# Turning the keys on VectorE instead of TensorE in a decode-attention kernel

## The chip, the cores and the metric

The kernel runs on one core of a Trainium2 chip. The core has TensorE (PE: matmuls and transposes, results into PSUM), VectorE (DVE), ScalarE (ACT), GpSimd (POOL) and the queues that issue transfers, here almost only SyncE's (SP). The metric is the device time of one execution in microseconds (us), the median of several runs; the profile is one execution of its own.

## The reference, cut to what matters

```python
def _A_ref(x, k_cache, v_cache, wq, wo):          # B=2, D=512, 32 query heads, 8 KV heads, Dh=128
    W = min(4096, max(256, Sk // 4))              # 4096: the last 4096 keys of 32768
    q = (x @ wq) ...                              # one position per batch entry
    k = jnp.repeat(k_cache[:, :, Sk - W:, :], 4, axis=1)
    v = jnp.repeat(v_cache[:, :, Sk - W:, :], 4, axis=1)
    p = _softmax(jnp.einsum("bhqd,bhkd->bhqk", q, k) * (Dh ** -0.5), axis=-1)
    return einsum("bhqk,bhkd->bhqd", p, v) ... @ wo
def _B_ref(x, W_gate, W_up, W_down):              # F = 1792
    gate = x @ W_gate; up = x @ W_up
    return (gate * (gate > 0) * up) @ W_down
xn = _layernorm(x)
return x + _A_ref(xn, ...) + _B_ref(xn, ...)
```

All data are float32. One token of each of two batch entries reads 4096 keys and 4096 values of eight KV heads, which with the weights makes 95 MB, each byte used once.

## The kernel before, in words

**Tiles and slots.** Attention goes in four groups g (batch entry b and half r of the KV heads, so four KV heads each), and each group in two pairs of heads, a = 0 and 1. One K tile and one V tile of 4 MB hold a pair (g, a). `load_kv` (L85) puts partition p = 2y + h: y counts 64 runs of 64 keys, h is the head of the pair; along a partition stand 64 keys (J) of 128 components. All large transfers (two halves of wq, W_gate, W_up, eight K, eight V, W_down, two parts of wo) go into one ring of four 4 MB slots (`load`, L69; RING = 4) and are issued in program order on SP's queue (L71, L449). A load therefore waits until the tile four loads before it has been read for the last time, and everything behind it on that queue waits with it. The order is: wq, wq, W_gate, W_up, K(0,0), K(0,1), then K(g,a), V(g-1,a) for g = 1 to 3, then V(3,0), V(3,1), W_down, wo.

**Program order.** `manual_schedule` (L66) keeps the instructions of each engine in the order in which the program emits them; there is no planner. An instruction that waits holds all that stand behind it on its engine.

**Keys and scores.** A score product needs the components of a key on the partitions. `transposes` (L248) turns a K tile on PE in 64 products of 128x128 with the identity (L256), four of them into one PSUM bank, and `evacuate` (L244) copies each bank to SBUF, alternately on ACT and DVE (L245), setting the two heads apart on the way. `scores` (L262) multiplies: per half tile s1, 2 heads x 4 column groups of 32 (L269), every one with 128 components, 32 query columns and 512 keys. The 32 columns of `qz` are zero except for the four query heads that belong there. All scores of a group gather in one PSUM bank, `ss[g]`.

**Softmax.** `softmax` (L275) is a generator whose steps `kwork` (L375) puts between the transposes of the next group's first K tile: maximum on DVE (L278), a transpose of it on PE, DVE steps, four small products `nm_ps` (L293), one exponential of 128x1024 on ACT (L302; each score is written twice), eight PE transposes of the probabilities (L313), two DVE products with the mask `own` that keeps a head's own half (L314), and the sums `lp` and their reciprocal (L320, L322).

**Values and the end.** `values` (L326) makes 16 products per V tile (L333) and a DVE mask (L339); `gather` (L346) adds pairs on PE, `finish` (L355) sums on DVE and divides, `spread_heads` (L363) moves heads to where the product with wo takes them. After the last group come W_down, wo, the sums and the store (L413 to L464).

Of the kernel before, what the change touches and what calls it, by code (L numbers as in the profile page):

```python
# [20 lines left out]
def kernel(  # L21
# [12 lines left out]
    nc = tc.nc  # L34
# [76 lines left out]
    NSLOT = C * S1  # L111
    qz = const.tile([P, NG, NSLOT * 36], F32, name="qz")
    nc.gpsimd.memset(qz, 0.0)
    ones = const.tile([1, 1], F32, name="ones")
# [7 lines left out]
    spread = const.tile([HR, NE, HR, NE], F32, name="spread")  # L122
    nc.gpsimd.memset(spread, 0.0)
    for e in range(NE):
        nc.gpsimd.tensor_copy(spread[:, e, :, e], ident[0:HR, 0:HR])
# [18 lines left out]
    by_h = const.tile([P, NP, HK], F32, name="by_h")  # L144
    nc.vector.tensor_reduce(
        out=by_h, in_=ident.rearrange("p (q a s k) -> p a k q s", q=Q, a=NP, s=S1), op=ALU.add, axis=AX.XY
    )

    half_of = const.tile([P, 2], F32, name="half_of")
    nc.vector.tensor_reduce(  # L150
        out=half_of, in_=ident.rearrange("p (y h) -> p h y", h=2), op=ALU.add, axis=AX.X
    )
    own = const.tile([P, 2, REP], F32, name="own")
    nc.vector.tensor_copy(own, half_of[:, :, None].to_broadcast([P, 2, REP]))

# [18 lines left out]
    xn = const.tile([B, D], F32, name="xn")  # L174
# [29 lines left out]
    for r in range(R):  # L204
        qs = work.tile([P, 512], F32, name=f"qs{r}", tag="qs")
        (nc.vector.tensor_copy if r else nc.scalar.copy)(qs, q_ps[r])
        qt = ps_kt.tile([P, REP, C, 16, B], F32, name=f"qt{r}", tag="kt")
        for i in range(REP):
            nc.tensor.transpose(  # L209
                qt[:, i].rearrange("p c s b -> p (c s b)"), qs[:, i * P:(i + 1) * P], ident  # L210
            )
        for b in range(B):
            dst = qz[:, r * B + b].rearrange("p (a s h k) -> p a s h k", a=NP, s=S1, h=2)
            for h in range(2):
                nc.vector.tensor_copy(  # L215
                    dst[:, :, :, h, 0:REP], qt[:, :, h::2, 0:S1, b].rearrange("p i a s -> p a s i")
                )

# [12 lines left out]
    gr = work.tile([P, FQ], F32, name="gr", tag="gr", bufs=1)  # L231
# [7 lines left out]
    HW = W // S1  # L239
    ss, pts, rls = {}, {}, {}  # L240
    kts, osb = {}, {}
    turn = [0]

    def evacuate(dst, src):  # L244
        (nc.vector.tensor_copy if turn[0] % 2 else nc.scalar.copy)(dst, src)  # L245
        turn[0] += 1

    def transposes(g, a, s1, kt_in):  # L248

        kt = ktp.tile([P, 2, HW], F32, name=f"kT{g}_{a}_{s1}", tag="kT")  # L250
        kts[g, a, s1] = kt
        for n in range(2 * Q):
            pk = ps_kt.tile([P, 512], F32, name=f"pk{g}_{a}_{s1}_{n}", tag="kt")
            for u in range(4):
                j = 8 * Q * s1 + 4 * n + u
                nc.tensor.transpose(pk[:, u * P:(u + 1) * P], kt_in[:, j * P:(j + 1) * P], ident)  # L256
            evacuate(
                kt[:, :, n * 256:(n + 1) * 256], pk.rearrange("p (y h) -> p h y", h=2),
            )
            yield  # L260

    def scores(g, a, s1):  # L262
        if (a, s1) == (0, 0):
            ss[g] = ps_s.tile([P, 512], F32, name=f"s{g}", tag="s")
        kt = kts.pop((g, a, s1))
        for h in range(2):
            n = (a * S1 + s1) * 2 + h
            for q in range(Q):
                nc.tensor.matmul(  # L269
                    ss[g][32 * q:32 * q + 32, :], qz[:, g, 32 * n:32 * n + 32],  # L270
                    kt[:, h, q * 512:(q + 1) * 512],
                    start=(a == 0 and s1 == 0 and h == 0), stop=(a == NP - 1 and s1 == S1 - 1 and h == 1),
                )

    def softmax(g):  # L275

        m = work.tile([P, 1], F32, name=f"m{g}", tag="m")
        nc.vector.tensor_reduce(out=m, in_=ss[g], op=ALU.max, axis=AX.X)  # L278
        yield
        mt = ps_1.tile([1, P], F32, name=f"mt{g}", tag="misc")  # L280
        nc.tensor.transpose(mt, m, ident)
        mx = work.tile([1, NP, HK], F32, name=f"mx{g}", tag="mx")
        nc.vector.tensor_reduce(
            out=mx, in_=mt.rearrange("p (q a s k) -> p a k q s", q=Q, a=NP, s=S1), op=ALU.max, axis=AX.XY
        )
        mb = work.tile([1, NP, S1, HK], F32, name=f"mb{g}", tag="mb")
        nc.vector.tensor_scalar(
            mb, mx[:, :, None, :].to_broadcast([1, NP, S1, HK]), -SCALE, None, op0=ALU.mult
        )
        yield  # L290
        nm_ps = ps_1.tile([P, 1], F32, name=f"nm_ps{g}", tag="misc")
        for q in range(Q):
            nc.tensor.matmul(  # L293
                nm_ps[32 * q:32 * q + 32, :], mb.rearrange("p a s k -> p (a s k)"), ones, start=True, stop=True
            )
        nm = work.tile([P, 1], F32, name=f"nm{g}", tag="nm")
        nc.vector.tensor_copy(nm, nm_ps)  # L297

        p = work.tile([P, 512, 2], F32, name=f"p{g}", tag="p", bufs=1)
        l = work.tile([P, 1], F32, name=f"l{g}", tag="l")  # L300
        both = ss[g][:, :, None].to_broadcast([P, 512, 2])
        nc.scalar.activation(p, both, AF.Exp, bias=nm, scale=SCALE, accum_out=l)  # L302
        yield
        yield
        yield

        pts[g] = work.tile([P, 2, Q * NP * S1, 4, HK], F32, name=f"pt{g}", tag="pt")
        pv = p.rearrange("r y h -> r (y h)")
        for jh in range(2):
            pp = ps_kt.tile([P, 4, P], F32, name=f"pp{g}_{jh}", tag="kt")  # L310
            for u in range(4):
                lo = (4 * jh + u) * P
                nc.tensor.transpose(pp[:, u], pv[:, lo:lo + P], ident)  # L313
            nc.vector.tensor_tensor(  # L314
                pts[g][:, jh].rearrange("p n u k -> p u n k"), pp.rearrange("p u (n k) -> p u n k", k=HK),
                own.rearrange("p h i -> p (h i)")[:, None, None, :].to_broadcast([P, 4, Q * NP * S1, HK]), op=ALU.mult,
            )
            yield
        lp = ps_1.tile([HR, 1], F32, name=f"lp{g}", tag="misc")
        nc.tensor.matmul(lp, by_h.rearrange("p a k -> p (a k)"), l, start=True, stop=True)  # L320
        rls[g] = work.tile([HR, 1], F32, name=f"rl{g}", tag="rl")
        nc.vector.reciprocal(rls[g], lp)  # L322

    ons = {}

    def values(g, a, v):  # L326
        o = ps_1.tile([P, 512], F32, name=f"o{g}_{a}", tag=f"o{a}")
        for s1 in range(S1):
            for jh in range(2):
                for q in range(Q):  # L330
                    n = (q * NP + a) * S1 + s1
                    lo = (8 * Q * s1 + 8 * q + 4 * jh) * P
                    nc.tensor.matmul(  # L333
                        o[32 * q:32 * q + 32, :],
                        pts[g][:, jh, n].rearrange("p u k -> p (u k)"), v[:, lo:lo + 512],
                        start=(s1 == 0 and jh == 0), stop=(s1 == S1 - 1 and jh == 1),
                    )
        ons[a] = work.tile([P, 4, P], F32, name=f"on{g}_{a}", tag="on")
# [16 lines left out]
    def finish(g):  # L355
# [5 lines left out]
        nc.vector.tensor_scalar(osb[r][:, b], od, rls[g], 2.0, op0=ALU.mult, op1=ALU.mult)  # L361

    def spread_heads(r):  # L363
        op = ps_1.tile([P, NJ, B], F32, name=f"op{r}", tag="misc")
        for e in range(NE):
            nc.tensor.matmul(  # L366
                op, spread[:, e].rearrange("h k e -> h (k e)"),
# [5 lines left out]
    pend = []  # L373

    def kwork(g, a, kt_in, others=()):  # L375

        others = list(others)
        for s1 in range(S1):
            for n, _ in enumerate(transposes(g, a, s1, kt_in)):
                if n > 1 and others and next(others[0], "end") == "end":  # L380
                    others.pop(0)
                if (a, s1, n) == (0, 0, 1) and pend:
                    scores(*pend.pop())
            if pend:
                scores(*pend.pop())
            pend.append((g, a, s1))
        for o in others:
            for _ in o:
                pass

    for a in range(NP):
        kwork(0, a, load_kv(k_cache, "k", 0, a))
    for g in range(1, NG):
        for a in range(NP):
            kt_in = load_kv(k_cache, "k", g, a)
            v_in = load_kv(v_cache, "v", g - 1, a)
            kwork(g, a, kt_in, [softmax(g - 1)] if a == 0 else [])
            if a:
                gather(g - 1, a - 1)
            elif g % B == 1 and g > 1:  # L400
                spread_heads((g - 2) // B)
            values(g - 1, a, v_in)
        gather(g - 1, NP - 1)
        finish(g - 1)
    g = NG - 1
    scores(*pend.pop())
    vin = [load_kv(v_cache, "v", g, a) for a in range(NP)]
    dw = load_down()
    for _ in softmax(g):
        pass  # L410
# [27 lines left out]
    for a in range(NP):  # L438
        values(g, a, vin[a])
        gather(g, a)  # L440
# [13 lines left out]
    yw = work.tile([P, D], F32, name="yw", tag="yw", bufs=1)  # L454
# [38 lines left out]
```

## Time and profile before

| what | before |
|---|---|
| median of 3 runs | 231.82 us (231.73 to 232.03) |
| the profiled execution | 231.71 us, its span 229.9 us |
| PE busy | 182.2 us in 1432 instructions |
| DVE busy | 73.3 us in 143 instructions |
| ACT busy | 46.6 us in 78 instructions |
| moved by DMA | 95.10 MB, mean 414 GB/s |
| mean granted TensorE clock | 0.925 |

The span goes from the first to the last instruction of the profiled execution; about 1.8 us of its time lie around it. Busy time is the time in which an engine had an instruction in work. In the lists of groups a row reads: line, engine, operation, tile written <- tiles read, partitions x elements, count | busy us, mean ns of one | idle us just before them and what ended it. The granted clock is the share of full speed that TensorE was given.

### The profile page before, as it was taken

The numbers are of one execution on the slowest core, as the hardware profiler recorded it, in microseconds if no ns is written. First come the engines' busy times: TensorE is split into PE (matmuls) and PEld (weight loads), VectorE is DVE, ScalarE is ACT, GpSimd is POOL, SyncE is SP. The second block draws the span as 40 slices with busy tenths as digits, with TensorE's granted clock in tenths as the row PEclk, the third lists the DMA queues.
The fourth block names the chain that finished last, engine by engine and source line by source line (L and its number), as shares of the span: only waits on it lengthen the run. The fifth ranks groups of instructions, "written<-read, shape, count | busy, mean of one in ns | idle before, by whom it ended". The sixth has DMA issues, their size and how long they took to land.

```text
span 229.9 us, 3250 instructions
## 1 busy us (share of the span) xinstructions
PE 182.2 (79%) x1432; PEld 96.0 (42%) x1432; DVE 73.3 (32%) x143; ACT 46.6 (20%) x78; POOL 3.8 (2%) x17
## 2 busy tenths in 40 slices
PE   0483970819999889998899699589999965889493
PEld 0430230219666573661583563248566213124011
DVE  2400021024444561641572441247244144111000
ACT  2000100004444550440351340025134002000001
POOL 6000000000000000000000000000000000000000
PEclk9998598576999999999999999889999996799799
DMA  7999999999999999999999999999999999999980
GB/s 274 456 433 391 464 409 466 399 445 450 422 408 450 436 410 423 448 428 413 439 450 419 416 446 442 410 422 456 425 410 436 445 422 430 428 445 405 420 339 14
DMA packets 3921, 95.10 MB, mean 414 GB/s; under 512 B 442, under 2 KB 450, under 8 KB 836
## 3 DMA queue, kind: packets, MB, share of 16 engines
q1 hardware_dynamic: 3896, 94.90, 96.4%
q8 instruction: 11, 0.18, 0.3%
q14 instruction: 2, 0.02, 0.0%
q10 hardware_dynamic: 12, 0.01, 0.0%
HBM read 94.90 MB, written 0.00 MB: 413 GB/s over the span
## 4 chain that ended last, share of the span: by engine, by line
PE 51%; DMA 41%; DVE 4%; ACT 2%; issue 1%; SPq 1%
DMA k<-in_A_k_cache_dram 25%; PE pk L256 23%; PE s L269 11%; DMA wo<-in_A_wo_dram 10%; PE o L333 9%; DMA wq<-in_A_wq_dram 5%; PE q_ps L198 3%; PE pp L313 2%; ACT p L302 2%; PE oa L350 2%; DVE kT L245 1%; PE op L366 1%; SPq L449 1%; DVE on L339 1%; PE nm_ps L293 0%
## 5 line engine op out<-in xcount | busy, mean ns | idle before, releaser
L256 PE MATMUL pk<-ident,k 128*128 128x128 f32 x512 | 67.3, 286 | 8.4 <-DMA k<-in_A_k_cache_dram 8.4
L256 PEld LDWEIGHTS pk<-ident,k 128*128 128x128 f32 x512 | 57.7, 146 | 24.6 <-issue 21.0
L245 ACT COPY kT<-pk 128x512 f32<-128x512 f32 x64 | 37.5, 586 | 100.1 <-PE pk L256 100.1
L245 DVE COPY kT<-pk 128x512 f32<-128x512 f32 x64 | 44.2, 691 | 37.9 <-PE pk L256 37.8
L333 PE MATMUL o<-v,pt 128*32 128x512 f32 x256 | 34.2, 627 | 0.0
L269 PE MATMUL s<-kT,qz 128*32 128x512 f32 x256 | 32.1, 607 | 0.0
L339 DVE TENSOR_TENSOR on<-o,own_u 128x512 f32<-128x512 f32 x8 | 5.5, 692 | 39.4 <-PE o L333 39.4
L333 PEld LDWEIGHTS o<-v,pt 128*32 128x32 f32 x256 | 8.9, 114 | 20.0 <-issue 19.9
L198 PE MATMUL q_ps<-wq,xnT 128*32 128x512 f32 x64 | 12.3, 940 | 4.3 <-DMA wq<-in_A_wq_dram 4.3
L269 PEld LDWEIGHTS s<-kT,qz 128*32 128x32 f32 x256 | 7.0, 111 | 13.2 <-issue 13.2
L350 PE MATMUL oa<-on,pick 128*16 128x512 f32 x16 | 8.2, 596 | 4.2 <-DVE on L339 4.2
L430 PE MATMUL yw_ps<-wo,oT 128*2 128x512 f32 x56 | 7.9, 703 | 3.9 <-DMA wo<-in_A_wo_dram 3.9
L186 PE MATMUL xt_ps<-rep,xn 2*128 2x32 f32 x16 | 3.7, 402 | 8.7 <-DVE rep L179 8.7
L225 PE MATMUL u_ps<-wu,xnT 128*32 128x448 f32 x32 | 5.2, 816 | 6.6 <-DMA wu<-in_B_W_up_dram 6.6
L198 PEld LDWEIGHTS q_ps<-wq,xnT 128*32 128x32 f32 x64 | 2.9, 163 | 12.9 <-issue 7.6
L313 PE MATMUL pp<-ident,p 128*128 128x128 f32 x32 | 5.5, 306 | 2.4 <-ACT p L302 1.5
L455 ACT COPY yw<-yw_ps 128x512 f32<-128x512 f32 x1 | 0.6, 586 | 33.3 <-PE yw_ps L430 33.3
L186 PEld LDWEIGHTS xt_ps<-rep,xn 2*128 2x128 f32 x16 | 3.6, 319 | 8.7 <-DVE rep L179 8.7
L302 ACT ACTIVATE p<-s,nm 128x1024 f32<-128x1024 f32 x4 | 4.5, 1115 | 13.0 <-DVE nm L297 12.9
L314 DVE TENSOR_TENSOR pt<-pp,own 128x512 f32<-128x512 f32 x8 | 5.5, 692 | 3.8 <-PE pp L313 3.7
L215 DVE COPY qz<-qt 128x16 f32<-128x16 f32 x8 | 0.8, 167 | 17.6 <-PE qt L209 17.6
L225 PEld LDWEIGHTS u_ps<-wu,xnT 128*32 128x32 f32 x32 | 1.3, 160 | 10.5 <-DMA wu<-in_B_W_up_dram 7.4
(72 smaller groups left out, 60.9 us busy)
## 6 DMA issues: line engine op xcount, KB each, us to landing
k<-in_A_k_cache_dram SPq DMA_DIRECT2D x8, 4096.0 KB, 29.1
v<-in_A_v_cache_dram SPq DMA_DIRECT2D x8, 4096.0 KB, 29.0
wq<-in_A_wq_dram SPq DMA_DIRECT2D x2, 4096.0 KB, 16.9
wo<-in_A_wo_dram SPq DMA_DIRECT2D x1, 4096.0 KB, 31.7
wg<-in_B_W_gate_dram SPq DMA_DIRECT2D x1, 3584.0 KB, 29.6
wu<-in_B_W_up_dram SPq DMA_DIRECT2D x1, 3584.0 KB
wd<-in_B_W_down_dram SPq DMA_DIRECT2D x1, 3584.0 KB
wo<-in_A_wo_dram SPq DMA_DIRECT2D x1, 2048.0 KB, 20.7
```

Of the source, the lines that this page charges most:

```text
L186: nc.tensor.matmul(xt_ps[:, v, kc, :], lhsT, rep16.rearrange("r s b -> r (s b)"), start=True, stop=True)
L198: nc.tensor.matmul(q_ps[r][32 * c:32 * c + 32, :], xnT[:, 0, kc, :], wqt[kc // 2][:, kc % 2, n * 512:(n + 1) * 512], start=(kc == 0), stop ...
L225: nc.tensor.matmul(dst[32 * c:32 * c + 32, :], xnT[:, 1, kc, :], wt[:, kc, c * FQ:(c + 1) * FQ], start=(kc == 0), stop=(kc == KC - 1),)
L245: (nc.vector.tensor_copy if turn[0] % 2 else nc.scalar.copy)(dst, src)
L256: nc.tensor.transpose(pk[:, u * P:(u + 1) * P], kt_in[:, j * P:(j + 1) * P], ident)
L269: nc.tensor.matmul(ss[g][32 * q:32 * q + 32, :], qz[:, g, 32 * n:32 * n + 32], kt[:, h, q * 512:(q + 1) * 512], start=(a == 0 and s1 == 0 ...
L302: nc.scalar.activation(p, both, AF.Exp, bias=nm, scale=SCALE, accum_out=l)
L313: nc.tensor.transpose(pp[:, u], pv[:, lo:lo + P], ident)
L333: nc.tensor.matmul(o[32 * q:32 * q + 32, :], pts[g][:, jh, n].rearrange("p u k -> p (u k)"), v[:, lo:lo + 512], start=(s1 == 0 and jh == 0 ...
L339: nc.vector.tensor_tensor(ons[a], o.rearrange("p (u d) -> p u d", u=4), own_u[:, :, None].to_broadcast([P, 4, P]), op=ALU.mult)
L350: nc.tensor.matmul(oa[g].rearrange("h u d -> h (u d)"), pick[:, 8 - 8 * a:24 - 8 * a], ons[a].rearrange("p u d -> p (u d)"), start=(a == 0 ...
L430: nc.tensor.matmul(yw_ps[32 * c:32 * c + B, :], lhsT, w, start=(n < Q), stop=(n >= wide - Q))
```

## The change

K tiles are no longer turned on PE. `nc.vector.transpose` turns blocks of 32x32 on DVE: each half of the components of a K tile (index mh) takes four instructions of 1024 elements per partition (CUT = 4), eight per K tile. A block keeps its 32 partitions, so after it a partition stands for one of 32 components in one of four runs of y (index x), and the 32 components of a block make only a quarter of the contraction. The score product is therefore block-diagonal: `qz` has 32 dense columns, 4 values of x by 2 tiles by 4 query heads, with non-zero rows only in the own quarter of the partitions, and 2 halves x 2 blocks x 2 heads x 2 halves of keys make 16 products per K tile, as before. The transposed elements leave DVE in the order key, block, y, head; the view of the output puts the two heads J*16 elements, 4096 bytes, apart.

The exponential becomes two of 64 partitions, each into its head's places of a tile `pz` whose others stay zero. The probabilities are turned by one DVE transpose (`turn`) and put in place by 16 copies of 32 partitions, alternately on ACT and DVE. `values` keeps its 16 products; its mask becomes a function of its own, put after `turn`. The steps `gather`, `finish` and `spread_heads` of one pair are called between the two halves of the next K tile. Some small tiles share memory, `spread` is built by one copy instead of eight, and `by_h` by two shorter sums; the order of the loads is as before.

```diff
+    qz = const.tile([P, NG, NB, NP, 2, 32], F32, name="qz")
+    pz = const.tile([P, JS, 32], F32, name="pz")
+    nc.gpsimd.memset(pz, 0.0)
...
+        for m in range(NB):
+            src = qt[32 * m:32 * m + 32, :, :, 0].rearrange("p i (t h) b -> p b t h i", h=2)
+            for x in range(Q):
...
+                (nc.vector.tensor_copy if x % 2 else nc.scalar.copy)(dst, src)
...
-            for u in range(4):
-                j = 8 * Q * s1 + 4 * n + u
-                nc.tensor.transpose(pk[:, u * P:(u + 1) * P], kt_in[:, j * P:(j + 1) * P], ident)
-            evacuate(
-                kt[:, :, n * 256:(n + 1) * 256], pk.rearrange("p (y h) -> p h y", h=2),
-            )
...
+    def keys(g, a, kt_in, between=()):
...
+        for mh in range(2):
+            kt = ktp.tile([P, 2, 2, J, 16], F32, name=f"kT{g}_{a}_{mh}", tag="kT")
+            src = kt_in.rearrange("p (j d) -> p j d", d=DH)[:, :, PK * mh:PK * mh + PK]
+            n = J // CUT
+            for c in range(CUT):
+                nc.vector.transpose(
+                    kt[:, :, :, c * n:(c + 1) * n].rearrange("p m h j i -> p j m i h"), src[:, c * n:(c + 1) * n]
                 )
+            for m in range(2):
+                for h in range(2):
+                    for s1 in range(S1):
+                        q = 2 * h + s1
+                        nc.tensor.matmul(
+                            ss[g][32 * q:32 * q + 32, :], qz[:, g, 2 * mh + m, a, h], kt[:, m, h, JS * s1:JS * s1 + JS],
...
+            if mh == 0:
+                for step in between:
+                    step()
...
+        for h in range(2):
+            o = slice(PK * h, PK * h + PK)
+            nc.scalar.activation(
+                pv[o, :, :, h], ss[g][o].rearrange("p (j i) -> p j i", j=JS), AF.Exp, bias=nm[o], scale=SCALE, accum_out=l[o],
             )
...
+    def turn(g):
+        pT = work.tile([P, JS, Q, NP, REP], F32, name=f"pT{g}", tag="pT", bufs=1)
+        nc.vector.transpose(pT.rearrange("p j x t k -> p (j x t k)"), pz.rearrange("p j s -> p (j s)"))
...
+                for x in range(Q):
+                    (nc.vector.tensor_copy if n % 2 else nc.scalar.copy)(
+                        pts[g][32 * x:32 * x + 32, :, s1, :, h], pT[q:q + 32, :, x].rearrange("p j t k -> p t j k")
                     )
...
     for a in range(NP):
-        kwork(0, a, load_kv(k_cache, "k", 0, a))
+        keys(0, a, load_kv(k_cache, "k", 0, a))
+    softmax(0)
+    turn(0)
+    late = []
     for g in range(1, NG):
         for a in range(NP):
             kt_in = load_kv(k_cache, "k", g, a)
             v_in = load_kv(v_cache, "v", g - 1, a)
+            keys(g, a, kt_in, late)
             if a:
+                softmax(g)
+            values(g - 1, a, v_in)
+            if a:
+                turn(g)
+            mask(g - 1, a)
+            late = [lambda g=g, a=a: gather(g - 1, a)]
+            if a:
+                late.append(lambda g=g: finish(g - 1))
+                if g % B == 0:
+                    late.append(lambda g=g: spread_heads((g - 1) // B))
```

More of the change, by code (lines that the diff above doesn't have):

```diff
@@ L120 @@
     oT = const.tile([P, R, NJ, B], F32, name="oT")
-    spread = const.tile([HR, NE, HR, NE], F32, name="spread")
+    spread = const.tile([HR, HR + 1, NE], F32, name="spread")
     nc.gpsimd.memset(spread, 0.0)
-    for e in range(NE):
-        nc.gpsimd.tensor_copy(spread[:, e, :, e], ident[0:HR, 0:HR])
+    nc.gpsimd.tensor_copy(spread[:, 0:HR, NE - 1], ident[0:HR, 0:HR])
     pick = const.tile([P, 24], F32, name="pick")
@@ L230 @@
     nc.scalar.copy(gs, g_ps)
-    gr = work.tile([P, FQ], F32, name="gr", tag="gr", bufs=1)
+    gr = gs
     nc.vector.scalar_tensor_tensor(gr, gs, 0.0, gs, op0=ALU.is_gt, op1=ALU.mult)
@@ L262, in scores @@
-    def scores(g, a, s1):
-        if (a, s1) == (0, 0):
-            ss[g] = ps_s.tile([P, 512], F32, name=f"s{g}", tag="s")
[L265 to L272, printed above, removed]
-                )
+    osb = {}
@@ L275, in softmax @@
+    ls = {}
     def softmax(g):
@@ L285, in softmax @@
         )
-        mb = work.tile([1, NP, S1, HK], F32, name=f"mb{g}", tag="mb")
+        mb = work.tile([1, 2, S1 * Q, TK], F32, name=f"mb{g}", tag="mb")
         nc.vector.tensor_scalar(
-            mb, mx[:, :, None, :].to_broadcast([1, NP, S1, HK]), -SCALE, None, op0=ALU.mult
+            mb, mx[:, :, None, :].to_broadcast([1, 2, S1 * Q, TK]), -SCALE, None, op0=ALU.mult
         )
-        yield
         nm_ps = ps_1.tile([P, 1], F32, name=f"nm_ps{g}", tag="misc")
[L292 to L295, printed above, removed]
+        nc.tensor.matmul(nm_ps, mb.rearrange("p h x k -> p (h x k)"), ones, start=True, stop=True)
@@ L308, in softmax @@
[L308 to L316, printed above, removed]
-            )
-            yield
+        l = ls[g] = work.tile([P, 1], F32, name=f"l{g}", tag="l")
@@ L396 @@
             v_in = load_kv(v_cache, "v", g - 1, a)
-            kwork(g, a, kt_in, [softmax(g - 1)] if a == 0 else [])
+            keys(g, a, kt_in, late)
             if a:
-                gather(g - 1, a - 1)
-            elif g % B == 1 and g > 1:
-                spread_heads((g - 2) // B)
+                softmax(g)
             values(g - 1, a, v_in)
-        gather(g - 1, NP - 1)
-        finish(g - 1)
+            if a:
[6 more added lines that the diff above has]
+                    late.append(lambda g=g: spread_heads((g - 1) // B))
+    for step in late:
+        step()
     g = NG - 1
-    scores(*pend.pop())
     vin = [load_kv(v_cache, "v", g, a) for a in range(NP)]
     dw = load_down()
-    for _ in softmax(g):
-        pass
     y_ps = ps_kt.tile([P, P], F32, name="y_ps", tag="kt")
```

105 lines of the change are left out of this document (40 added, 65 removed).

## The prediction

> **What bounds the kernel now.** I read the page first: span, busy times, transfers.
>
> ```profile
> span 229.9 us, 3250 instructions
> PE 182.2 (79%) x1432; PEld 96.0 (42%) x1432; DVE 73.3 (32%) x143; ACT 46.6 (20%) x78; POOL 3.8 (2%) x17
> ...
> q1 hardware_dynamic: 3896, 94.90, 96.4%
> ```
>
> PE looks like the bound, but SP's queue keeps the sixteen DMA engines busy for 96.4% of the span. What is missing, 3.6% of 229.9 or 8.3 us, lies mostly at the two ends, as the table of 5-us windows shows (its last columns are granted clock, DMA share, GB/s):
>
> ```profile
> 0.00:5.00 5.00, 0.00 (x0) 0.00 (x0) 0.63 (x5) 1.28 (x1) 3.77 (x17) 1.00 0.69 243
> ...
> 225.00:230.00 5.00, 1.54 (x40) 0.72 (x40) 0.29 (x1) 0.47 (x1) 0.00 (x0) 0.95 0.02 7
> ```
>
> These two windows lack 0.31 x 5 + 0.98 x 5 = 6.5 of the 8.3 us. At most 1.8 us, 0.8%, could be won in between, whatever PE does. The list of DMA issues tells why PE's load does not hold the transfers up:
>
> ```profile
> k<-in_A_k_cache_dram SPq DMA_DIRECT2D x8, 4096.0 KB, 29.1
> ```
>
> A K tile lands 29.1 us after its issue. 4.19 MB at the mean of some 430 GB/s between the ends take 9.75 us, so two tiles always stand in front of the one just issued: PE frees slots two tiles early. The kernel is bound by its transfers, with PE some 19 us ahead of them. A group (two K and two V tiles) has 39 us to pass.
>
> **What the change removes.** The list of groups:
>
> ```profile
> L256 PE MATMUL pk<-ident,k 128*128 128x128 f32 x512 | 67.3, 286 | 8.4 <-DMA k<-in_A_k_cache_dram 8.4
> ...
> L245 DVE COPY kT<-pk 128x512 f32<-128x512 f32 x64 | 44.2, 691 | 37.9 <-PE pk L256 37.8
> L245 ACT COPY kT<-pk 128x512 f32<-128x512 f32 x64 | 37.5, 586 | 100.1 <-PE pk L256 100.1
> ...
> L314 DVE TENSOR_TENSOR pt<-pp,own 128x512 f32<-128x512 f32 x8 | 5.5, 692 | 3.8 <-PE pp L313 3.7
> L339 DVE TENSOR_TENSOR on<-o,own_u 128x512 f32<-128x512 f32 x8 | 5.5, 692 | 39.4 <-PE o L333 39.4
> L313 PE MATMUL pp<-ident,p 128*128 128x128 f32 x32 | 5.5, 306 | 2.4 <-ACT p L302 1.5 <-DVE kT L245 0.8
> ```
>
> PE loses 67.3 + 5.5 = 72.8 us, ACT 37.5, DVE 44.2 + 5.5 = 49.7. None of it stood on the path that sets the end, so removing it is worth at most the 1.8 us above.
>
> **What it adds: 64 DVE transposes of 1024 elements.** Four groups of two K tiles with eight instructions each. The trace has one DVE transpose; beside it I read other DVE rows to learn what an element costs.
>
> ```profile
> L235 DVE STREAM_TRANSPOSE hT<-hh 128x448 f32<-128x448 f32 x1 | 0.9, 936 | 0.0
> ...
> L234 DVE TENSOR_TENSOR hh<-gr,u_ps 128x448 f32<-128x448 f32 x1 | 0.6, 621 | 10.5 <-PE u_ps L225 10.5
> ...
> L138 DVE TENSOR_REDUCE fold<-ident 128x32 f32<-128x128 f32 x1 | 0.4, 358 | 0.0
> ...
> L461 DVE COPY yo<-y_ps 128x128 f32<-128x128 f32 x1 | 0.3, 292 | 13.5 <-PE y_ps L434 13.5
> L134 DVE TENSOR_REDUCE own_u<-ident 128x4 f32<-128x128 f32 x1 | 0.3, 275 | 0.0
> ```
>
> Elements in order: 692 ns for 512 and 621 for 448, so 71/64 = 1.11 ns each and 0.124 us fixed. The transpose: (936 - 124)/448 = 1.81 ns each. Its input (L235) steps 14 floats from element to element, its output is dense. The two sums of 128 elements show the same: L134 reads runs of eight and takes 275 ns, L138 steps 32 floats at every element and takes 358. So a jump at every element costs DVE about 0.7 ns more each when it reads. The change reads in runs of 64 but writes each element 4096 bytes from the one before, heads alternating. The trace has no DVE write of that kind. Bounds for one instruction: dense 0.124 + 1024 x 1.11 = 1.26 us; scaled whole from the transpose row 936 x 1024/448 = 2.14 us. I take 0.124 + 1024 x 1.81 = 1.98 us, because the nearest row is the same operation, with a jump at every element on one side. Back to back they start a little closer:
>
> ```profile
> 84.09 0.69 DVE L314 TENSOR_TENSOR pt<-pp,own 128x512 f32<-128x512 f32 x1 [0.24 <-PE pp L313]
> 84.70 0.68 DVE L245 COPY kT<-pk 128x512 f32<-128x512 f32 x1
> ```
>
> 0.61 us apart at 0.69 us each, so 0.08 less: 1.90 us, with ends of 1.18 and 2.06. A group needs 16 of them: 30.4 us (18.9 if dense).
>
> [...]
>
> **What waits on DVE.** DVE takes its work in program order, so where it waits for PE the next transposes wait too. The durations from the chain of waits and the windows:
>
> ```profile
> 66.32 1.85 PE s L269 x16
> ...
> 88.46 3.43 PE o L333 x32
> ...
> 195.01 5.52 PE o L333 x32
> ```
>
> ```profile
> 190.00:195.00 5.00, 2.60 (x30) 1.67 (x33) 2.25 (x6) 1.21 (x2) 0.00 (x0) 0.70 0.98 420
> 195.00:200.00 5.00, 5.00 (x33) 1.17 (x32) 0.00 (x0) 0.00 (x0) 0.00 (x0) 0.62 0.98 418
> ```
>
> Eight score products take 1.85 us and sixteen value products 3.43 us at full clock; after a stretch in which PE was busy 2.60 of 5 us the clock fell to 0.62 and the values took 5.52, 1.61 times as long. By that ratio the scores would take 3.0. In the change PE has only 1.85 us of scores per four transposes, so it will often be throttled; in its long bursts it recovers. I take 2.4 us for scores and 4.5 for values, between these ends. The softmax from the same chain:
>
> ```profile
> 188.23 0.70 DVE m L278
> ...
> 190.40 1.22 ACT p L302 x2
> ```
>
> 2.2 us from the maximum to the start of the exponential. That is 1.22 us for 1024 elements; two of 512 lie between 1.22 and 2.44, I take 1.6. So per group, on DVE:
>
> - 16 transposes 30.4
> - the mask of the first V tile, queued behind the second half's scores and the values: 2.4 + 4.5 + 0.7 = 7.6; the next K tile's transposes stand behind it
> - softmax: the wait for scores 2.4, then 2.2, exponential 1.6: 6.2
> - `turn`: one dense transpose 1.2, eight copies of 256 elements at 0.124 + 256 x 1.11 ns less 0.08 = 0.33: 2.6 (ACT's eight, by its 586 ns for 512 some 0.4 each, go beside them; only the values wait for the last): 3.8
> - reciprocal and second mask 0.9
>
> That is 48.9 us for g = 1. From g = 2 on, `finish` between the halves waits for scores and `gather` (2.4 + 0.5) and works 1.0: 3.9 more, 52.8; g = 3 has `spread_heads` too, about 2.1: 54.9. g = 0 has neither mask nor gather: 30.4 + 6.2 + 3.8 + 0.2 = 40.6. It starts when the first K tile has landed:
>
> ```profile
> 19.16 31.70 DMA k<-in_A_k_cache_dram
> ```
>
> 50.9, with the step to the engine 51.0. Sum: 51.0 + 40.6 + 48.9 + 52.8 + 54.9 = 248.2 us, where the last probabilities are in place; before that point was 195.0, where the last values began (quoted above). From there to the end of the span it took 34.9 us, including waits for wo; I take 30 without most of them, since wo, whose slots come free with the last values, then lands only as fast as it is used. 278.2 us of span, plus 1.8 around it as in the execution before: **280.0 us**. That execution (231.71) lies 0.1 below the median, so nothing is corrected.
>
> Every group now costs DVE more than the 39 us of its transfers, so the slot of a K tile comes free later each time, SP waits in front of the next load with all loads behind it, and the DMA engines stand idle.
>
> **The small edits** cost nothing: 32 small copies into `qz` go on ACT and DVE while both wait for weights (at most the 0.36 us of L138 each, 16 per engine, under 6 us, ahead of the first K tile at 51); larger POOL memsets end before it too; the shared tiles are read for the last time long before they are written again. If that cover were gone, they would cost up to those 6 us at the start.
>
> **The rivals.**
> 1. *Dense-rate writes.* If DVE writes alternating places as fast as dense ones, 64 x 0.72 = 46.1 us go: 248.2 - 46.1 = 202.1, 7 us later than the 195.0 of before, and 202.1 + 30 + 1.8 = 233.9 us. A slower clock (3.0 and 5.5) adds, over nine waits for scores and three for values, 9 x 0.6 + 3 x 1.0 = 8.4 us: 242. For it: the reading side is dense, and only reads are shown to suffer. [...]
> 2. *Hidden.* Dense writes and a full clock: scores 1.85, values 3.43 take off 9 x 0.55 + 3 x 1.07 = 8.2 us: 193.9, before 195.0. Then the transfers set the end as now: 231.8, no change. Against it: the 0.62 above, with PE idling more than it does today.
> 3. *Faster.* As 2, and PE's and ACT's lower traffic lets the DMA engines fill their gaps in mid-span. Worth at most 1.8 us, 230.0; half of it, 230.9. It decides only if DVE's chain stays under 39 us per group, which needs dense writes.
> 4. *The change does not unload PE.* The score products keep their number and size, so a throttled PE could become the bound; but 182 - 73 = 109 us of PE work, even at 1.61 times, is 176 of 230. I give this nothing of its own.
>
> **How the numbers follow.** A difference under 0.2% is about what a measurement of this kernel cannot tell from none. The scattered writes have 0.62, rival 1 0.18, rival 2 0.09, rival 3 0.11. So slower 0.80, same 0.09, faster 0.11. The main case's own range: a full clock and 0.65 ns for a jump, as the two sums have it ((358 - 275)/128; 1.85 us per transpose, 3 us less in all), give 280 - 3 - 8 = 269; 2.06 us per transpose gives 290, a slow clock a little more. The range that holds 8 in 10 reaches down to rivals 1 and 2: 231 to 291.
>
> **What would show it.** In the profile after, the group of DVE transposes (64 at 1024 elements): 1.98 us each if right, 1.26 under rival 1. DVE busy about 64 x 1.9 + 30 = 150 us and PE about 110; gaps in the DMA row from about 100 us on; SP waiting for DVE transposes; clock under 0.9. Wrong would be: the DMA row at 9 throughout, or a mean under 1.4 us.

## The result and the profile after

The changed kernel takes 278.83 us (median of four runs, 277.32 to 280.69), the kernel before, timed beside it, 231.93 us (231.73 to 232.2). The ratio is 1.2025, with an interval of 1.1949 to 1.2102: slower by a fifth. The profiled execution took 278.39 us, its span is 276.4 us and its mean granted clock 0.757. Where a run below is called single, its time is one execution; the four of the changed kernel itself lie 3.4 us apart.

The head of the page after, where each digit is the busy share of one of 40 slices of the span in tenths:

```profile
span 276.4 us, 2113 instructions
...
PE 157.5 (57%) x864; PEld 39.5 (14%) x864; DVE 156.1 (56%) x178; ACT 26.6 (10%) x70; POOL 3.7 (1%) x11
...
PEclk9997888558695567859757577777575775979999
DMA  7999999999999906997995289779920999799960
...
q1 hardware_dynamic: 3896, 94.90, 82.1%
```

No engine is busy for even six tenths of the span, and the transfers, at 96.4% before, are down to 82.1%. With nothing full, the waits have to tell: the chain that ended last goes through DVE for 51% of the span, PE for 26% and the transfers for 16%. The DMA row, which had 9 nearly throughout, now falls to 0 or 2 in three places ahead of the end. From its 5-us windows (the last columns are granted clock, DMA share and GB/s):

```profile
100.00:105.00 5.00, 2.57 (x10) 0.14 (x2) 5.00 (x3) 0.00 (x0) 0.00 (x0) 0.84 0.00 0
...
150.00:155.00 5.00, 1.65 (x2) 0.18 (x2) 5.00 (x4) 0.00 (x0) 0.00 (x0) 0.74 0.00 0
...
205.00:210.00 5.00, 1.19 (x11) 1.07 (x10) 3.78 (x4) 0.00 (x0) 0.00 (x0) 0.70 0.00 0
```

Three times nothing moves at all for five microseconds, while DVE (the third pair of columns) works through twice and for 3.78 us the third time. Why is in the waits of SP's queue (us in total, times, longest) and in the landing of the K tiles; what DVE does is in the list of groups:

```profile
SPq L71 <- DVE kT L252: 138.5, 8, 25.0
```

```profile
k<-in_A_k_cache_dram SPq DMA_DIRECT2D x8, 4096.0 KB, 19.1
```

```profile
L259 PE MATMUL s<-kT,qz 128*32 128x512 f32 x256 | 77.8, 935 | 81.0 <-DVE kT L252 80.6
L252 DVE STREAM_TRANSPOSE kT<-k 128x1024 f32<-128x1024 f32 x64 | 115.9, 1935 | 4.8 <-DMA k<-in_A_k_cache_dram 4.8
...
L332 DVE TENSOR_TENSOR on<-o,own_u 128x512 f32<-128x512 f32 x8 | 5.5, 692 | 30.5 <-PE o L323 30.5
...
L298 DVE STREAM_TRANSPOSE pT<-pz 128x1024 f32<-128x1024 f32 x4 | 5.0, 1246 | 8.3 <-ACT pz L292 8.3
```

SP waits 138.5 us, in eight waits, for the DVE transposes that free a K slot. A K tile lands 19.1 us after its issue where it took 29.1, because fewer loads stand in front of it: the lead over the transfers is used up. The two transpose rows are the same instruction on the same number of elements: writing `pT` in order takes 1246 ns, writing `kT` with the heads 4096 bytes apart 1935 ns. PE waits 80.6 us for DVE, and DVE waits 30.5 us for the values in front of the masks, 22.35 us of it in three waits (6.81, 8.30 and 7.24). One group, g = 2, on DVE (start, duration, and in brackets the idle time before and what ended it):

```profile
137.64 7.27 DVE L252 STREAM_TRANSPOSE kT<-k 128x1024 f32<-128x1024 f32 x4
148.67 0.68 DVE L353 TENSOR_REDUCE od<-oa 16x128 f32<-16x512 f32 x1 [3.76 <-PE oa L343]
149.39 0.28 DVE L354 TENSOR_SCALAR osb<-od,rl 16x128 f32<-16x128 f32 x1
149.59 7.26 DVE L252 STREAM_TRANSPOSE kT<-k 128x1024 f32<-128x1024 f32 x4
165.15 0.69 DVE L332 TENSOR_TENSOR on<-o,own_u 128x512 f32<-128x512 f32 x1 [8.30 <-PE o L323]
165.76 14.47 DVE L252 STREAM_TRANSPOSE kT<-k 128x1024 f32<-128x1024 f32 x8
183.66 0.69 DVE L272 TENSOR_REDUCE m<-s 128x1 f32<-128x512 f32 x1 [3.43 <-PE s L259]
...
187.69 1.25 DVE L298 STREAM_TRANSPOSE pT<-pz 128x1024 f32<-128x1024 f32 x1 [1.76 <-ACT pz L292]
188.97 2.38 DVE L305 COPY pt<-pT 32x256 f32<-32x256 f32 x8
191.36 0.15 DVE L312 RECIPROCAL rl<-lp 16x1 f32<-16x1 f32 x1
191.53 0.69 DVE L332 TENSOR_TENSOR on<-o,own_u 128x512 f32<-128x512 f32 x1
192.14 1.94 DVE L252 STREAM_TRANSPOSE kT<-k 128x1024 f32<-128x1024 f32 x1
```

The group lasts from 137.64 to 192.14, 54.5 us, against the 39 us that its transfers need. 29.0 us of it are transposes of keys (7.27 + 7.26 + 14.47) and 18.1 us are waiting, the longest time in front of the mask; the remaining 7 us are DVE's other work. The mask's wait delays more than itself: the next transposes stand behind an instruction that PE must first reach.

### The profile page after: what moved, and what is told of

It reads as the page before. It is cut to its first block, busy times and chain, and to the rows that moved or that the text cites. A ratio compares the mean times of both kernels' runs of the same rounds, so it can differ in the third digit from the quotient of the medians.

```text
span 276.4 us, 2113 instructions
## 1 busy us (share of the span) xinstructions
PE 157.5 (57%) x864; PEld 39.5 (14%) x864; DVE 156.1 (56%) x178; ACT 26.6 (10%) x70; POOL 3.7 (1%) x11
## 3 DMA queue, kind: packets, MB, share of 16 engines
q1 hardware_dynamic: 3896, 94.90, 82.1%
## 4 chain that ended last, share of the span: by engine, by line
DVE 51%; PE 26%; DMA 16%; ACT 3%; issue 2%; ACTq 0%
DVE kT L252 41%; DMA k<-in_A_k_cache_dram 11%; PE s L259 10%; PE o L323 7%; DMA wq<-in_A_wq_dram 5%; PE yw_ps L411 3%; DVE pt L305 3%; PE q_ps L195 2%; ACT pz L292 2%; DVE pT L298 2%; DVE on L332 2%; PE op L359 1%; PE oa L343 1%; DVE m L272 1%; DVE od L353 1%
## 5 line engine op out<-in xcount | busy, mean ns | idle before, releaser
L259 PE MATMUL s<-kT,qz 128*32 128x512 f32 x256 | 77.8, 935 | 81.0 <-DVE kT L252 80.6
L252 DVE STREAM_TRANSPOSE kT<-k 128x1024 f32<-128x1024 f32 x64 | 115.9, 1935 | 4.8 <-DMA k<-in_A_k_cache_dram 4.8
L323 PE MATMUL o<-v,pt 128*32 128x512 f32 x256 | 40.9, 712 | 0.0
L259 PEld LDWEIGHTS s<-kT,qz 128*32 128x32 f32 x256 | 11.3, 143 | 140.6 <-DVE kT L252 109.4
L332 DVE TENSOR_TENSOR on<-o,own_u 128x512 f32<-128x512 f32 x8 | 5.5, 692 | 30.5 <-PE o L323 30.5
L292 ACT ACTIVATE pz<-s,nm 64x512 f32<-64x512 f32 x8 | 5.8, 720 | 136.5 <-DVE nm L286 136.4
L343 PE MATMUL oa<-on,pick 128*16 128x512 f32 x16 | 12.5, 877 | 2.9 <-DVE on L332 2.9
L305 ACT COPY pt<-pT 32x256 f32<-32x256 f32 x32 | 12.9, 402 | 5.6 <-DVE pT L298 5.2
L298 DVE STREAM_TRANSPOSE pT<-pz 128x1024 f32<-128x1024 f32 x4 | 5.0, 1246 | 8.3 <-ACT pz L292 8.3
L305 DVE COPY pt<-pT 32x256 f32<-32x256 f32 x32 | 9.1, 285 | 0.5
L359 PE MATMUL op<-osb,spread 16*128 16x32 f32 x32 | 3.9, 273 | 1.1 <-DVE osb L354 1.1
## 6 DMA issues: line engine op xcount, KB each, us to landing
k<-in_A_k_cache_dram SPq DMA_DIRECT2D x8, 4096.0 KB, 19.1
```

Source lines behind the costliest of these rows:

```text
L252: nc.vector.transpose(kt[:, :, :, c * n:(c + 1) * n].rearrange("p m h j i -> p j m i h"), src[:, c * n:(c + 1) * n])
L259: nc.tensor.matmul(ss[g][32 * q:32 * q + 32, :], qz[:, g, 2 * mh + m, a, h], kt[:, m, h, JS * s1:JS * s1 + JS], start=(a == 0 and mh == 0 ...
L292: nc.scalar.activation(pv[o, :, :, h], ss[g][o].rearrange("p (j i) -> p j i", j=JS), AF.Exp, bias=nm[o], scale=SCALE, accum_out=l[o],)
L298: nc.vector.transpose(pT.rearrange("p j x t k -> p (j x t k)"), pz.rearrange("p j s -> p (j s)"))
L305: (nc.vector.tensor_copy if n % 2 else nc.scalar.copy)(pts[g][32 * x:32 * x + 32, :, s1, :, h], pT[q:q + 32, :, x].rearrange("p j t k -> p ...
L323: nc.tensor.matmul(o[32 * q:32 * q + 32, :], pts[g][:, a, s1, j:j + 4].rearrange("p u h k -> p (u h k)"), v[:, lo:lo + 512], start=(s1 == ...
```

## The experiments

Three theories stood. Theory 1 is the prediction's: DVE's chain in program order sets the time, and the jump at every written element makes it this long. Theory 2 is a rival that the profile of before could not exclude: a float transpose of 1024 elements costs 1.9 us wherever it writes. Theory 3: PE sets the time, since the granted clock fell from 0.925 to 0.757. The edits are against the changed kernel unless said otherwise, and the runs of the kernel before on the same chips had medians between 231.56 and 231.77 us.

### Dense writes

```diff
-            kt = ktp.tile([P, 2, 2, J, 16], F32, name=f"kT{g}_{a}_{mh}", tag="kT")
+            kt = ktp.tile([P, J, 2, 16, 2], F32, name=f"kT{g}_{a}_{mh}", tag="kT")
-                    kt[:, :, :, c * n:(c + 1) * n].rearrange("p m h j i -> p j m i h"), src[:, c * n:(c + 1) * n]
+                    kt[:, c * n:(c + 1) * n], src[:, c * n:(c + 1) * n]
...
- kt[:, m, h, JS * s1:JS * s1 + JS]
+ kt[:, JS * s1:JS * s1 + JS, m, :, h]
```

DVE writes in order; the jump goes to the score products, which now read every second float.

> The turned keys are written in the order in which VectorE makes them (key, block, y, head: dense), and the score products read one head at every second float instead. Theory 1 (VectorE's in-order chain sets the time, and most of what it gained in length is the jump of 4096 bytes at every written element): a transpose falls from the 1.94 us of the changed kernel to about 1.25, as the dense transpose of the probabilities has it (1246 ns), some 0.65 us less for each of 64, so about 42 us less: 233 to 241 us, unless the products pay for reading every second float. Theory 2 (a float transpose of 1024 elements costs 1.9 us wherever it writes): no change, 278 us. Theory 3 (PE and its throttled clock set the time, VectorE only waits): little change, above 265 us.

Measured: 234.93 us (234.08 to 235.34), ratio to the kernel before 1.0143 (1.0126 to 1.016). Its group of transposes, eight of them in DVE's timeline, and its DMA row:

```profile
L252 DVE STREAM_TRANSPOSE kT<-k 128x1024 f32<-128x1024 f32 x64 | 73.2, 1208 | 5.5 <-DMA k<-in_A_k_cache_dram 5.5
```

```profile
96.22 9.12 DVE L252 STREAM_TRANSPOSE kT<-k 128x1024 f32<-128x1024 f32 x8
```

```profile
DMA  7999999999999999999999999999999999999940
```

In a row one takes 9.12/8 = 1.14 us instead of 1.81 (14.47/8): 64 x 0.67 = 42.9 us, and the span became 276.4 - 232.1 = 44.3 us shorter. The products that now read every second float pay next to nothing for it: the maximum behind them waits 2.06 to 2.15 us, where it waited 2.03 us in three groups of four. Theory 2 falls: a float transpose can be had for 1.2 us. Theory 3 falls as the main cause too: PE has the same products to do, only read in another order, and 44 of the 47 us went. (The granted clock rose too, to 0.831; what a raised clock is worth by itself follows below.)

### Half as many, twice as long

`CUT = 2` instead of 4: 32 transposes of 2048 elements.

> Half as many transposes of 2048 elements each, still scattered. Theory 1: the cost is per element, so one takes about 3.7 us and only the fixed part of 32 instructions goes, some 0.07 us each or 2 us in all; the first products of each half start later: 275 to 280 us. If instead the fixed part of an instruction were what is expensive (0.5 us or more), 16 us or more would go: below 263 us.

Measured: 277.3 us, a single run.

```profile
L252 DVE STREAM_TRANSPOSE kT<-k 128x2048 f32<-128x2048 f32 x32 | 115.9, 3735 | 4.9 <-DMA k<-in_A_k_cache_dram 4.8
```

(3735 - 1935)/1024 = 1.76 ns per element and 1.935 - 1.024 x 1.76 = 0.13 us fixed. The cost is in the elements, as expected.

### Another length of the jump

One kernel with the heads 64 bytes apart (order block, key, head, y), one with 16,384 bytes (one constant tile for everything, `kall`, with the head ahead of the half).

```diff
+            kt = ktp.tile([P, 2, J, 2, 16], F32, name=f"kT{g}_{a}_{mh}", tag="kT")
+                    kt[:, :, c * n:(c + 1) * n].rearrange("p m j h i -> p j m i h"), src[:, c * n:(c + 1) * n]
...
+ kt[:, m, JS * s1:JS * s1 + JS, h]
```

```diff
+    kall = const.tile([P, 2, 2, 2, J, 16], F32, name="kall")
+            kt = kall[:, :, mh].rearrange("p h m j i -> p m h j i")
```

> The two heads are written 64 bytes apart instead of 4096; still no two neighbouring elements in a row. Theory 1, cost of a jump at every element whatever its length: a transpose stays at 1.9 us and the time at 278 us. If a write port joined elements that fall close together, it would go towards 1.25 us and the time towards 237 us; if short jumps cost more than long ones, 2.6 us and some 320 us.

> The two heads are written 16384 bytes apart. Theory 1, cost of a jump whatever its length: 1.9 us per transpose, 278 us. If the cost came from two places that share a bank and 16384 bytes led to another one, it would go to 1.25 us and the time to some 237 us.

Measured: 275.42 and 277.51 us, a single run each. The group of transposes of the one and of the other:

```profile
L252 DVE STREAM_TRANSPOSE kT<-k 128x1024 f32<-128x1024 f32 x64 | 112.7, 1881 | 4.8 <-DMA k<-in_A_k_cache_dram 4.8
```

```profile
L253 DVE STREAM_TRANSPOSE kall<-k 128x1024 f32<-128x1024 f32 x64 | 115.9, 1940 | 4.9 <-DMA k<-in_A_k_cache_dram 4.8
```

1881, 1935 and 1940 ns for 64, 4096 and 16,384 bytes, against 1208 in order: what costs is that the next float isn't the neighbour; how far away it is, between 64 and 16,384 bytes, makes 59 ns.

### The mask out of the way

The masks are called in `late`, between the halves of the next K tile, so that the transposes of the first half stand ahead of them. The one that matters is that of the first V tile, in front of which DVE waited. The scattered writes stay.

```diff
-            mask(g - 1, a)
-            late = [lambda g=g, a=a: gather(g - 1, a)]
+            late = [lambda g=g, a=a: mask(g - 1, a), lambda g=g, a=a: gather(g - 1, a)]
```

> The changed kernel with its scattered writes; only the mask of each V tile and with it VectorE's wait for the values move behind the first half of the next K tile, where the values are long done. Theory 1 (in-order chain): the three waits of 6.81, 8.30 and 7.24 us before the mask of the first V tile go, and some 22 us with them: 255 to 259 us. If the transposes alone set the time (64 x 1.81 = 116 us do not fill the span, so something else would have to take their place), it stays above 270 us.

Measured: 262.48 us, a single run. All three waits in front of masks are gone, 22.35 us together, but DVE's path became only 15.8 us shorter (from 245.9 to 230.1 for the last mask that follows a reciprocal). Two rows of its timeline:

```profile
160.90 0.69 DVE L332 TENSOR_TENSOR on<-o,own_u 128x512 f32<-128x512 f32 x1
...
172.60 0.69 DVE L272 TENSOR_REDUCE m<-s 128x1 f32<-128x512 f32 x1 [3.75 <-PE s L259]
```

The mask has no wait, and the maximum waits 3.75 us for the scores where it waited 3.43. Over the four groups these waits went from 2.03, 2.03, 3.43, 2.03 to 3.32, 3.75, 3.75, 3.75, 5 us more. The granted clock in these four waits was 1.00, 1.00, 0.58 and 1.00; in the clock row of the page with the late mask the slices of 6.5 us in which they end have 7, 5, 5 and 5 tenths, and the same products took longer. The 255 to 259 us expected left that out.

### Both edits

> Dense writes and the late mask together. Theory 1: VectorE's chain, which reached the last probabilities at 199 us with dense writes, loses 5.59 + 7.29 + 6.13 = 19 us of waits and is ready at about 180, well before the 195.0 of the kernel before; then the transfers alone set the end: 231 to 232.5 us, the same as before within 0.3%, though PE has 70 us less to do. If PE's load had held the transfers up before, it would now be faster: 229 us or less. If VectorE's chain still counts, 233 us or more.

Measured: 230.35 us (230.24 to 230.66), ratio 0.9945 (0.9932 to 0.9959): half a per cent below the kernel before, little but clear of the noise, and below the 231 to 232.5 us expected. Lines of its page:

```profile
DMA  7999999999999999999999999999999999999991
...
q1 hardware_dynamic: 3896, 94.90, 96.9%
q8 instruction: 7, 0.11, 0.2%
...
k<-in_A_k_cache_dram SPq DMA_DIRECT2D x8, 4096.0 KB, 29.4
```

With DVE out of the way the kernel is bound by its transfers again, and a K tile lands 29.4 us after its issue, as it did before (29.1). DVE's last reciprocal is done at about 189 us, before the 195.0 of the kernel before, though not at the 180 expected: DVE itself now waits 8.7 us for K tiles to land. The place of the mask is worth 234.93 - 230.35 = 4.6 us beside dense writes.

### The clock of PE

Idle products with a result that nobody uses, to keep the clock up. First three of 128x512 behind the scores of each half:

```diff
+            fp = ps_kt.tile([P, 512], F32, name=f"fp{g}_{a}_{mh}", tag="kt")
+            for _ in range(3):
+                nc.tensor.matmul(fp, ident, qz[:, 0].rearrange("p m t h c -> p (m t h c)"), start=True, stop=True)
```

> The changed kernel with three more products of 128x512 behind the scores of each half K tile, whose result nobody reads: work for TensorE that keeps its clock up while VectorE turns keys. Theory 1 with the throttle as a part: the granted clock rises from 0.76 to 0.9 or more, the waits for scores (3.6 us at the low clock) fall towards 1.95 and those for values to 3.5, some 8 to 10 us in all: 267 to 272 us. Theory 3 (the throttled clock is the main cause): 250 us or less. If the clock did not matter at all: 278 us or, since the products stand in front of other work on PE, more.

Measured: 292.26 us, a single run, clock 0.829, against 267 to 272 expected. It says little about the clock, since the fill itself stood in front of PE's next work:

```profile
84.52 0.28 DVE L279 TENSOR_REDUCE mx<-mt 1x16 f32<-1x128 f32 x1 [2.17 <-PE mt L277]
...
115.60 0.69 DVE L335 TENSOR_TENSOR on<-o,own_u 128x512 f32<-128x512 f32 x1 [8.49 <-PE o L326]
```

The small transpose of the maximum had been waited for 0.36 us, now 2.17, and the masks waited 8.49, 10.69 and 8.38 us. So the fill was put into the time in which PE has nothing to do: after each of the first three transposes of a half, two products of 128x256 that read what that transpose wrote.

```diff
+                if c == 0:
+                    fp = ps_kt.tile([P, 512], F32, name=f"fp{g}_{a}_{mh}", tag="kt")
+                if c < CUT - 1:
+                    for m in range(2):
+                        nc.tensor.matmul(
+                            fp[:, 256 * m:256 * m + 256], ident, kt[:, m, 0, c * n:(c + 1) * n], start=True, stop=True
+                        )
```

> The changed kernel (scattered writes, early mask) with idle products put where they cannot stand in front of other work: after each of the first three transposes of a half tile, two products of 128x256 that read what it has just written, 1.7 us at the low clock, less than the 1.81 us to the next transpose. Theory 1 with the throttle as a part: PE is warm when the scores come, so these take 1.95 us instead of 3.6 and the values 3.5 instead of 4.6; of the 276.4 us of span some 8 to 10 go: 267 to 271 us. Theory 3 (the clock is the main cause): 250 us or less. If the clock did not matter: 277 to 279 us.

Measured: 269.45 us, a single run, clock 0.87. Its score products and one of its masks:

```profile
L266 PE MATMUL s<-kT,qz 128*32 128x512 f32 x256 | 39.9, 618 | 0.0
```

```profile
160.59 0.69 DVE L339 TENSOR_TENSOR on<-o,own_u 128x512 f32<-128x512 f32 x1 [5.46 <-PE o L330]
```

The records of the score products (two to a product) took 618 ns instead of 935, and all three masks waited 5.46 us instead of 6.81, 8.30 and 7.24. The low clock is thus real, and raising it to 0.87 was worth 278.8 - 269.5, about 9 us of the 47; it lengthens the waits of DVE's chain and is not what sets the time in the main.

### Where the gain of the kernel with both edits comes from

Half a per cent lies between it and the kernel before. One row in which the pages differ has 0.11 MB of instructions on q8, where the kernel before has

```profile
q8 instruction: 11, 0.18, 0.3%
```

Theory A: instructions are fetched by the same transfers as the weights, and the kernel with fewer of them (2114 against 3250) takes less from these. Theory B: it comes from elsewhere, the end of the kernel for one. Three kernels, each on top of both edits. The first issues 1136 tiny memsets on POOL, the second 288 products of one column on PE (26 behind the scores of each first half and 20 behind the second half of a = 0), the third three idle products behind the last `spread_heads`, to raise the clock for the product with wo.

```diff
+    scratch = const.tile([1, 1], F32, name="scratch")
+    for _ in range(1136):
+        nc.gpsimd.memset(scratch, 0.0)
```

```diff
+            if mh == 0 or a == 0:
+                fp = ps_kt.tile([1, 1], F32, name=f"fp{g}_{a}_{mh}", tag="kt")
+                for _ in range(26 if mh == 0 else 20):
+                    nc.tensor.matmul(fp, ident[:, 0:1], ident[:, 0:1], start=True, stop=True)
```

```diff
+    fp = ps_kt.tile([P, 512], F32, name="fp", tag="kt")
+    for _ in range(3):
+        nc.tensor.matmul(fp, ident, qz[:, 0].rearrange("p m t h c -> p (m t h c)"), start=True, stop=True)
```

> The dense, late-mask kernel with 1136 tiny memsets on GpSimd into one unused float: as many instructions more as the kernel before has over the changed one (3250 and 2113 in the profiles; the page of before shows 0.18 MB of instruction transfers, the others 0.11), on an engine that nobody waits for. Theory A (the 0.55% won against the kernel before come from fewer instruction bytes on the engines that carry the weights): it goes back to the time of the kernel before, ratio 0.999 to 1.001, with 0.18 MB in the instruction queue. Theory B (they come from somewhere else, PE's products or the end of the kernel): the ratio stays at 0.993 to 0.996.

> The dense, late-mask kernel with 288 products of one column, whose result nobody reads, behind the scores of most half tiles: float32 products take four PE instructions each, so about 1150 instructions more, this time on the engine whose instructions the change had removed; 1 to 2 us of PE time at a place, inside the next half's transposes. Theory A (the gain of 0.55% over the kernel before is fewer instruction bytes beside the weights): 0.18 MB in the instruction queue again and the time back at the kernel before, ratio 0.998 to 1.002. Theory B (the gain comes from the end or from PE's products): ratio 0.993 to 0.997.

> The dense, late-mask kernel with three products of 128x512, whose result nobody reads, between spread_heads and the products with wo, 2.6 us in a wait of 3.6 us for wo: the 56 records with wo, which took 9.03 us at a falling clock, take some 6.2. If the end of that kernel is set by PE's clock there: up to 1.5 us less, 229 us or a little more, ratio 0.988 to 0.993. If the last pieces of wo set it: within 0.3 us of 230.35, ratio 0.993 to 0.996.

Measured: 234.79 us, ratio 1.0136 (1.0119 to 1.0153), for the memsets; 231.98 us, 1.001 (1.0001 to 1.0018), for the products; 230.51 us, 0.9949 (0.9938 to 0.9961), for the raised clock. The kernel with the memsets, instruction rows of its page and a row of its DVE timeline; then the kernel with the PE products, two lines of its page:

```profile
q8 instruction: 7, 0.11, 0.2%
q14 instruction: 11, 0.09, 0.1%
```

```profile
131.31 4.62 DVE L252 STREAM_TRANSPOSE kT<-k 128x1024 f32<-128x1024 f32 x4 [4.67 <-DMA k<-in_A_k_cache_dram]
```

```profile
span 229.7 us, 3266 instructions
...
q8 instruction: 11, 0.18, 0.3%
```

The PE products bring the 11 packets and 0.18 MB of the kernel before back, and with them its time: what was won is gone. DVE's chain was not held up by them (the last reciprocal stands at 186.94 us, at 188.97 without them). The end of the kernel is not it: with the clock raised the products with wo took 6.6 us instead of 9.0 in all, and the time stayed. The memsets, fetched over another queue (q14: 11 packets and 0.09 MB, against 2 and 0.02 in the kernel with both edits), went beyond either expectation: they cost 4.4 us (1.0136 - 0.9945 of 231.77). The K tile that DVE can turn from 131.31 us in the row above had landed by 128.54 us in the kernel with both edits.

Where the time goes shows at the end of the kernel, in the products that wait for the first part of wo. The kernel with both edits, then the one with the PE products (shortest, median and longest record in ns, then the first and the last start in us):

```profile
L410 PE MATMUL yw_ps<-wo,oT x56: 592/765/1057, 214.9 to 223.3; 128*2 128x512 f32 x56
```

```profile
L414 PE MATMUL yw_ps<-wo,oT x56: 592/592/1057, 216.2 to 224.2; 128*2 128x512 f32 x56
```

They start at 214.9 and 216.2 us; in the kernel before it was 216.4, with the memsets 218.9. The weights themselves kept the DMA engines busy equally long in all four: 96.9% of 228.7, 96.5% of 229.7, 96.4% of 229.9 and 95.4% of 232.5 us are 221.6 to 221.8 us. So more instructions went with a later landing and not with more engine time for the weights. That the fetches make the landing late, by holding up one engine while the others run ahead, would fit, but the views do not show which engine carried them. Nor is the price settled: 0.07 MB more went with 1.5 us in the one (231.98 - 230.51, on one chip) and 4.4 us in the other. An estimate: at 430/16 = 26.9 GB/s for one of the sixteen DMA engines (the kernel before moves 430 GB/s from 100 to 190 us), 0.07 MB take 2.6 us if one engine carries them all and 0.2 us if all share them. The 1.5 us lie between these ends, the 4.4 us beyond them; the memsets may cost in another way besides, and the PE products add 13 us of PE work as well as instructions (149.8 us busy against 136.8). Theory B loses its example, the end of the kernel; Theory A fits the kernel with the PE products and is not proved. This stays open.

## Why the prediction was right

The forecast was 280.0 us, by the scattered writes on DVE's chain; measured 278.83, and undoing the scattered writes alone took 44 of the 47 us back, so the mechanism is shown. That the sum came within 1.2 us is in part luck: terms within it were off by several us, in both directions. By its steps:

- **The transposes.** 1.98 us each were taken from the one transpose with jumps on its reading side; measured 1.94. In a row one takes 1.81 us, not 1.90, so sixteen took 29.0 us instead of 30.4. Dense they took 1.21 us, 1.14 in a row, where the prediction's lower bound had 1.26 and 1.18. Per element that is 1.1 ns in order (1.14 us for 1024) and 1.8 ns scattered (1.81 us); the step from 1024 to 2048 elements gave 1.76 ns each.
- **The groups.** Predicted 40.6, 48.9, 52.8 and 54.9 us, measured 40.0 (50.7 to 90.7), 46.9, 54.5 and 54.4; the last probabilities in place at 246.5 instead of 248.2, then 29.9 us to the end for 30. Terms within the groups were off in both directions: the scores in front of the maximum, taken at 2.4 us, were waited for 2.03 us three times and 3.43 once, since the clock differs from burst to burst; the waits before the masks, 2.4 + 4.5 = 6.9 by the sum, were 6.81, 8.30 and 7.24; the wait in `finish` was 3.76 instead of 2.9; the copies of `turn` took 2.38 for 2.6. One term was missing: a table load of 1.28 us in front of the first exponential, on the path of g = 0. The 30 us for the end were a choice without a sum behind it, and hit by luck.
- **PE.** "PE about 110" busy was wrong: 157.5 us. The products were counted at full clock; at the low one a record of the score products took 935 ns in the mean, where it had taken 607. It cost little here, as PE waits 80.6 us for DVE anyway, but the stated way by which the clock acts, through the waits for scores and values, is the one that gave back 9 us with the paced fill.
- **The transfers.** Gaps in the DMA row from about 100 us on, SP waiting for DVE transposes, a clock under 0.9: all there.
- **The small edits.** The 16 copies on each of ACT and DVE into `qz` end before 38 us, and DVE turns the first K tile at 50.71, when it has landed: they cost nothing.
- **The rivals.** The first gave 233.9 us for dense writes, and the kernel with dense writes took 234.93. That is closer than its terms: the last probabilities were in place at 199.2 instead of 202.1 us, and from there to the end it took 32.9 us instead of 30. The third gave 230.9 for a chain that stays under the transfers, and the kernel with both edits took 230.35. Its reason, less traffic of PE and ACT, is not what the runs point to: 288 products of one column, which read next to no data but brought 0.07 MB more on q8, took the gain away.

## What to carry to other kernels

Where an instruction reads and writes in different orders, put the jump on the side that bears it: here the products read every second float and the maximum behind them waited 2.06 to 2.15 us instead of 2.03, while DVE paid 0.67 us per 1024 elements (1.81 instead of 1.14) for writing so. On an engine that works in order, sum up what it does per step, its waits included, and compare that with the transfers of the step; a busy share of 56% said nothing here. An instruction that must wait for another engine belongs behind the work that doesn't, and what that gained here was less than the wait that vanished, 15.8 of 22.35 us, as the waits behind it grew.

## What the runs showed of the hardware

- DVE's price for writing elsewhere at each element hardly differed over three distances: a transpose of 1024 floats took 1881 ns with 64 bytes, 1935 with 4096 and 1940 with 16,384, and 1208 in order.
- A few products of no use, placed in the pauses of PE, raised the mean granted clock from 0.757 to 0.87 and made the whole kernel 9 us faster, while another fill, behind the scores, raised it to 0.829 and made the kernel 13 us slower.
- Instructions are part of the traffic: 0.07 MB of them more, beside 95 MB of weights, went with 1.5 us more, some nine times their share of the bytes (0.07/95 of 230 us is 0.17 us). That the fetching itself is the cause fits the runs but is not shown apart from the work that the instructions do.
